# A gated-attention and two-MLP kernel: the second weight set's remainder moves from TensorE to VectorE, and two rules of its planner change

## The chip, the cores and the metric

One core of one Trainium2 chip. The metric is the device time of one execution in microseconds. Three engines matter: TensorE (PE; its weight loads are a row of their own, PEld), VectorE (DVE) and ScalarE (ACT). SyncE (SP) only issues the DMAs.

## The reference

The input is a batch of 4, with 8 heads, 768 steps and a head width of 48. A linear recurrence with a complex gate comes first, then two MLPs one after the other, all in float32.

```
a_re, a_im = a_re * scale, a_im * scale      # scale = min(|a|, 0.999) / (|a| + 1e-6)
for t in range(768):
    S_re, S_im = ar*S_re - ai*S_im + outer(k[t], v[t]), ar*S_im + ai*S_re
    y[t] = q[t] @ S_re
x = y as (3072, 384)
h = x @ w_in;   x   = (h * tanh(softplus(h))) @ w_out        # w_in 384 x 2048
h = x @ w2_in;  out = (h * clip(h + 3, 0, 6) / 6) @ w2_out
```

## The kernel before

**Numbers as pairs.** Every float32 factor of the MLPs is held as two float16 tiles, `hi` (the rounded value) and `lo` (the remainder), and each product is three float16 matmuls (hi·hi, hi·lo, lo·hi). This holds for the weights (`w1i`, `w1o`, `w2i`, `w2o`: first and second MLP, in and out) as for the activations (`x_hi`/`x_lo`, `gh`/`gl`).

**Weights (`weights`, L828 to L848).** The weights arrive as float64 bit patterns and are converted in pieces of 128x512, 24 pieces for the first set (`w1i`, `w1o`) and 24 for the second (`w2i`, `w2o`). One piece takes a DMA, ACT L840, DVE L841 and L842 (they make the float32 value `tf`), ACT L843 (`hi`), then PE L845 and L846 and ACT L847 for the remainder:

```
        act(out=hi, in_=tf, func=AF.Copy, scale=s * 2.0 ** -128)
        pw = ps_h.tile([128, 512], F32, name="pw", tag="ph")
        mm(pw, small, tf, start=True, stop=False)
        mm(pw, minus[:, idx % 2], hi, start=False, stop=True)
        act(out=lo, in_=pw, func=AF.Copy, scale=s / SWO)
```

`small` and `minus` are scaled identities, so that `pw` is the value minus `hi`. For the second set the value lies in a tile `wt` of one buffer.

**Blocks and stages.** The 3072 tokens are cut into 12 blocks of 256. For a block b there are: E`b` (`elementwise`, `spread`, `tail`: the gates' running products on DVE and ACT in the tiles `inp`, `tq` and `pp`, then 12 DMAs that lay the results out anew as `rq` and `rk`); C`b` (`chunks`: two chunks of 128 steps, each with the transposes `pk`, the scores `psc`, in `advance` the state update `pu`, in `second` the outputs `py` in two parts (scores by values at L785, queries by the old state `sd` at L791), and in `turn` the transposes `pst`; at last `x1conv` forms `x_hi` and `x_lo`); the first MLP's layer (0, b) and the second's (1, b). A layer is 8 pairs of column tiles; a pair is 18 matmuls into `ph` (L889), one ScalarE/VectorE treatment (`act1` with four ACT steps and DVE L912, or `act2` with one ACT step and DVE L919), the split into `gh` (ACT L925) and `gl` (DVE L926), and 18 matmuls out (L902).

**Order of the layers.** (0,0), (0,1), (1,0), (0,2), (1,1), (0,3), and so on. The second set of weights is converted during (0,0) and (0,1); it is needed from (1,0) on.

**What sets the order.** `survey` and `plan` arrange all instructions on each engine: `survey` gives each a cost and lists what it must wait for, `plan` sweeps over them forwards and backwards, and the resulting row of each engine is fixed. Two of its rules matter here. `runs` are groups of matmuls with 64 output partitions (`pu`, `py`) that are kept together as one piece; a group ends where the tile written or the kind of the first operand changes (the test at L332). And `lag` (L384) is the time that the plan leaves between an instruction and one that waits for it: 900 ns behind a DMA, 6000 ns more where the waiting one is part of the weights' range check (label "G").

Of the kernel before, what the change touches and what calls it, by code (L numbers as in the profile page):

```python
# [10 lines left out]
F32 = mybir.dt.float32  # L11
# [3 lines left out]
AF = mybir.ActivationFunctionType  # L15
ALU = mybir.AluOpType
# [23 lines left out]
SLACK = {}  # L40
AHEAD = 0.17
MARGIN = 6000.0
SIGN = -2147483648
BUT_SIGN = 0x7FFFFFFF
LOW3 = 2.0 ** -29 * (1.0 - 2.0 ** -20)
# [5 lines left out]
SWO = 2.0 ** 5  # L51
# [192 lines left out]
def survey(instructions, first, labels):  # L244
# [14 lines left out]
    ops, label, tags = [], [], [x[1] for x in labels]  # L259
# [8 lines left out]
            label.append(tags[j])  # L268
    n = len(ops)
    preds = [dict() for _ in range(n)]  # L270
    runs, where, stage = [], {}, {}
    seen, users, rows = {}, {}, {}
    cost, issue, dma, port = [0.0] * n, [0.0] * n, [False] * n, [False] * n
    for k, i in enumerate(ops):
        aps = [(x, False) for x in i.ins if hasattr(x, "bass_ap")] + [(x, True) for x in i.outs if hasattr(x, "bass_ap")]
        tiles = [(x.bass_ap, mybir.dt.size(x.dtype), wr) for x, wr in aps]
        out = tiles[-1][0]
        for ap, width, wr in tiles:
            name = ap.tensor.name
            tag = getattr(ap.tensor, "tag", None)  # L280
            if tag is None:
                continue
            key = tag.split("_")[0] if not tag.startswith("x2_") else tag[:5]
            wr = wr or key in ("oa", "oB")
            whole = key in ("ph", "oa", "oB", "pa", "td")
            box = (0, 128, 0, 1 << 30)
            if not whole:
                p0, lo = divmod(ap.offset, ap.ap[0][0])
                lo += sum(s * (c - 1) for s, c in ap.ap[1:] if s < 0)
                hi = lo + sum(abs(s) * (c - 1) for s, c in ap.ap[1:]) + 1  # L290
                box = (p0, p0 + ap.ap[0][1], lo * width, hi * width)
            if name not in seen:
                seen[name], users[name] = [], []
                row = rows.setdefault(tag, [])
                if row:
                    preds[k][users[row[-1]][0]] = ops[users[row[-1]][0]].engine != i.engine
                row.append(name)
                old = len(row) - 1 - bufs.get(key, 1)
                if old >= 0:
                    for p in users[row[old]]:  # L300
                        preds[k][p] = True
            if users[name]:
                first_use = users[name][0]
                if first_use != k:
                    preds[k].setdefault(first_use, ops[first_use].engine != i.engine)
            users[name].append(k)
            keep = []
            for b, p, pw in seen[name]:
                if (wr or pw) and b[0] < box[1] and box[0] < b[1] and b[2] < box[3] and box[2] < b[3] and p != k:
                    preds[k][p] = preds[k].get(p, False) or pw or ops[p].engine != i.engine  # L310
                if wr and p != k and box[0] <= b[0] and b[1] <= box[1] and box[2] <= b[2] and b[3] <= box[3]:
                    continue
                if not wr and not pw and b == box and tag.startswith("w"):
                    continue
                keep.append((b, p, pw))
            keep.append((box, k, wr))
            seen[name] = keep
        free = max(size(ap.ap) for ap, _, _ in tiles)
        if "DMA" in type(i).__name__:
            dma[k] = True  # L320
            count = math.prod(c for _, c in out.ap)
            issue[k] = 450.0 if out.ap[0][1] > 32 else 625.0
            cost[k] = count * tiles[-1][1] / (360.0 if min(adjacent(ap) * w for ap, w, _ in tiles) >= 2048 else 175.0)
        elif i.engine == tensor:
            passes = 1 if tiles[0][1] == 2 else 2 if i.is_transpose else 4
            cost[k] = passes * size(out.ap) / 2.4 + (2.0 if passes == 1 else 8.0)
            if out.ap[0][1] == 64:
                cost[k] = 115.0
                last = runs[-1][-1] if runs else -1
                if runs and label[last] == label[k] and out.tensor.name == where[last] and stage[last] == tiles[0][0].tensor.tag.split("_")[0]:  # L330
                    runs[-1].append(k)
                else:  # L332
                    runs.append([k])
                    cost[k] += 250.0
                where[k], stage[k] = out.tensor.name, tiles[0][0].tensor.tag.split("_")[0]
        elif i.engine == vector:
            fast = type(i).__name__ == "InstMemset" or (type(i).__name__ == "InstTensorScalarPtr" and len(tiles) == 2)
            steps = max(abs(ap.ap[-1][0]) * w for ap, w, _ in tiles)
            cost[k] = 66.0 + free / (1.92 if fast else 0.96) * (1.5 if steps >= 32 else 1.0)
            sb = [ap for ap, _, wr in tiles if not wr and getattr(ap.tensor, "tag", "").split("_")[0] not in ("ph", "oa", "oB", "pa")]  # L340
            port[k] = len(sb) >= 2 or fast
        elif i.engine == scalar:
            psum = tiles[0][0].tensor.tag.split("_")[0] in ("ph", "oa", "oB", "pa")
            cost[k] = (51.0 if psum else 94.0) + 93.0 * sum(size(ap.ap) == 1 for ap, _, _ in tiles) + free / 1.2
        else:
            cost[k] = 46.0 + free * 2.083
            port[k] = True
# [4 lines left out]
def plan(ops, label, preds, cost, issue, dma, port, runs):  # L352
# [5 lines left out]
    last = -1  # L358
    for k in range(n):
        if ops[k].engine == tensor and label[k][0] == "M":  # L360
            if last >= 0:
                chain[last] = k
            last = k
# [19 lines left out]

    def lag(p, k):  # L384
        if dma[p]:
            return 900.0 + (MARGIN if label[k] == "G" else 0.0)
        return after[ops[p].engine] if preds[k][p] and not (ops[p].engine == ops[k].engine == tensor) else 0.0

    rank = [0.0] * n
# [88 lines left out]
def fast_path(ctx, tc, a, out, flag):  # L478
    nc = tc.nc
    mm = nc.tensor.matmul  # L480
    act = nc.scalar.activation
    tt = nc.vector.tensor_tensor
    ts = nc.vector.tensor_scalar
    stt = nc.vector.scalar_tensor_tensor
# [12 lines left out]
    ps_h = ctx.enter_context(tc.tile_pool(name="ps_h", bufs=PHB, space=PSUM))  # L497
# [7 lines left out]
            name=nc.get_next_instruction_name(),  # L505
# [42 lines left out]
    minus = const.tile([128, 2, 128], F16, name="minus")  # L548
    small = const.tile([128, 128], F32, name="small")
# [278 lines left out]
    def weights(idx, nm, s, o):  # L828
# [9 lines left out]
        tf = t.bitcast(F32)  # L838
        hi, lo = W[nm][0][:, o:o + 512], W[nm][1][:, o:o + 512]
# [1 line left out]
        stt(t, hw, 3, lw, op0=ALU.logical_shift_left, op1=ALU.bitwise_or)  # L841
        stt(t, hw, BUT_SIGN, t, op0=ALU.bitwise_or, op1=ALU.bitwise_and)  # L842
        act(out=hi, in_=tf, func=AF.Copy, scale=s * 2.0 ** -128)  # L843
        pw = ps_h.tile([128, 512], F32, name="pw", tag="ph")
        mm(pw, small, tf, start=True, stop=False)  # L845
        mm(pw, minus[:, idx % 2], hi, start=False, stop=True)  # L846
        act(out=lo, in_=pw, func=AF.Copy, scale=s / SWO)  # L847
        yield  # L848

    def weight_guard():  # L850
# [11 lines left out]
    stage = iter(range(24))  # L862
# [116 lines left out]
    start = len(nc.cur_bb.bb.instructions)  # L979
# [133 lines left out]
```

## Time and profile before

| | us |
|---|---|
| median of 3 runs | 1038.88 |
| lowest and highest of them | 1034.57, 1039.21 |
| the profiled execution | 1037.71 |
| its span in the trace | 1035.8 |
| TensorE busy in it | 968.7 |
| VectorE busy | 800.5 |
| ScalarE busy | 675.2 |

The span is what the trace covers; 1.9 us lie around it. Busy times are unions over an engine's own instructions, and the three engines work side by side, so that they add up to more than the span. An engine's share of the whole span is a mean over stages that differ: the weights' conversion and the first blocks stand at the start, and from (1,0) on blocks and layers repeat.

### The profile page before, as it was taken

The numbers are of one execution on the slowest core, as the hardware profiler recorded it, in microseconds if no ns is written. First come the engines' busy times: TensorE is split into PE (matmuls) and PEld (weight loads), VectorE is DVE, ScalarE is ACT, GpSimd is POOL, SyncE is SP. The second block draws the span as 40 slices with busy tenths as digits, with TensorE's granted clock in tenths as the row PEclk, the third lists the DMA queues.
The fourth block names the chain that finished last, engine by engine and source line by source line (L and its number), as shares of the span: only waits on it lengthen the run. The fifth ranks groups of instructions, "written<-read, shape, count | busy, mean of one in ns | idle before, by whom it ended". The sixth has DMA issues, their size and how long they took to land.

```text
span 1035.8 us, 21145 instructions
## 1 busy us (share of the span) xinstructions
PE 968.7 (94%) x8719; PEld 817.9 (79%) x8719; DVE 800.5 (77%) x1455; ACT 675.2 (65%) x1181; POOL 0.9 (0%) x7
## 2 busy tenths in 40 slices
PE   3576889999999999999999999999999999999998
PEld 1144577788888888887888888888887988988887
DVE  7978779979699695895797996895994996654532
ACT  7865789955856846846747747747647747637532
POOL 0000000000000000000000000000000000000000
PEclk9888999999999999999999999999999999999999
DMA  9771854550615126029027146327237227222000
GB/s 357 287 137 45 157 169 143 135 106 24 119 37 100 43 68 112 1 68 166 3 91 158 53 114 151 98 89 156 84 108 131 83 85 155 85 69 77 22 16 19
DMA packets 58681, 106.64 MB, mean 103 GB/s; under 512 B 6482, under 2 KB 40018, under 8 KB 58578
## 3 DMA queue, kind: packets, MB, share of 16 engines
q1 hardware_dynamic: 53586, 100.50, 39.0%
q10 hardware_dynamic: 4992, 4.72, 1.4%
q8 instruction: 70, 1.15, 0.5%
q14 instruction: 33, 0.27, 0.1%
HBM read 80.35 MB, written 4.79 MB: 82 GB/s over the span
## 4 chain that ended last, share of the span: by engine, by line
PE 60%; DVE 16%; ACT 10%; DMA 9%; SPq 2%; issue 2%; ACTq 0%; DVEq 0%
PE ph L889 25%; PE oa L902 16%; PE oB L902 8%; DMA rk<-tq 5%; PE psc L739 3%; PE pw L845 2%; SPq L713 2%; PE py L785 1%; DMA rq<-inp 1%; DVE gl L926 1%; DMA yr<-yr 1%; PE py L791 1%; ACT s L909 1%; DVE s L919 1%; DVE tq L682 1%
## 5 line engine op out<-in xcount | busy, mean ns | idle before, releaser
L926 DVE TENSOR_TENSOR gl<-s,gh 128x512 f16<-128x512 f32 x192 | 131.9, 687 | 53.4 <-ACT gh L925 52.8
L925 ACT ACTIVATE gh<-s 128x512 f16<-128x512 f32 x192 | 120.1, 625 | 76.0 <-DVE s L919 64.2
L889 PE MATMUL ph<-x_hi,w1i_hi 128*128 128x256 f16 x576 | 158.4, 276 | 6.3 <-ACT x_hi L817 3.7
L889 PE MATMUL ph<-x_lo,w1i_hi 128*128 128x256 f16 x576 | 158.6, 276 | 0.2 <-DVE x_lo L818 0.2
L889 PE MATMUL ph<-x_hi,w1i_lo 128*128 128x256 f16 x576 | 158.3, 275 | 0.0
L889 PE MATMUL ph<-x_hi,w2i_hi 128*128 128x256 f16 x576 | 157.1, 273 | 0.0
L889 PE MATMUL ph<-x_hi,w2i_lo 128*128 128x256 f16 x576 | 157.1, 273 | 0.0
L889 PE MATMUL ph<-x_lo,w2i_hi 128*128 128x256 f16 x576 | 157.1, 273 | 0.0
L889 PEld LDWEIGHTS <-w1i_hi 128*128 128x128 f16 x1152 | 113.9, 99 | 23.8 <-issue 8.5
L902 PEld LDWEIGHTS <-w1o_hi 128*128 128x128 f16 x1152 | 113.2, 98 | 20.6 <-issue 6.2
L902 PEld LDWEIGHTS <-w2o_hi 128*128 128x128 f16 x1152 | 112.2, 98 | 16.2 <-issue 4.0
L889 PEld LDWEIGHTS <-w2i_hi 128*128 128x128 f16 x1152 | 111.9, 98 | 14.7 <-issue 2.7
L918 ACT ACTIVATE s<-ph,half 128x512 f32<-128x512 f32 x96 | 65.5, 682 | 80.7 <-PE ph L889 80.6
L902 PE MATMUL oa<-gl,w1o_hi 128*128 128x256 f16 x384 | 105.1, 274 | 4.2 <-DVE gl L926 4.0
L902 PE MATMUL oa<-gh,w1o_hi 128*128 128x256 f16 x384 | 105.2, 274 | 3.2 <-ACT gh L925 3.2
L902 PE MATMUL oa<-gl,w2o_hi 128*128 128x256 f16 x384 | 104.7, 273 | 0.7 <-DVE gl L926 0.7
L902 PE MATMUL oa<-gh,w1o_lo 128*128 128x256 f16 x384 | 105.0, 273 | 0.0
L902 PE MATMUL oa<-gh,w2o_hi 128*128 128x256 f16 x384 | 104.7, 273 | 0.0
L902 PE MATMUL oa<-gh,w2o_lo 128*128 128x256 f16 x384 | 104.7, 273 | 0.0
L919 DVE SCALAR_TENSOR_TENSOR s<-s,ph 128x512 f32<-128x512 f32 x96 | 65.5, 682 | 43.1 <-ACT s L918 42.8
L912 DVE SCALAR_TENSOR_TENSOR s<-s,ph 128x512 f32<-128x512 f32 x96 | 65.6, 684 | 42.6 <-ACT s L911 42.1
L908 ACT ACTIVATE s<-ph 128x512 f32<-128x512 f32 x96 | 56.4, 588 | 24.2 <-PE ph L889 20.8
(153 smaller groups left out, 2076.7 us busy)
## 6 DMA issues: line engine op xcount, KB each, us to landing
wst<-in_w2i_dram SPq DMA_DIRECT2D x24, 512.0 KB
wst<-in_w2o_dram SPq DMA_DIRECT2D x24, 512.0 KB
rq<-inp SPq DMA_DIRECT2D x72, 128.0 KB
rk<-tq SPq DMA_DIRECT2D x72, 128.0 KB
inp<-in_ga_dram SPq DMA_DIRECT2D x11, 768.0 KB
inp<-in_qk_dram SPq DMA_DIRECT2D x11, 768.0 KB
vt<-in_vt_dram SPq DMA_DIRECT2D x24, 256.0 KB
wst<-in_w1i_dram SPq DMA_DIRECT2D x12, 512.0 KB
```

Of the source, the lines that this page charges most:

```text
L682: tt(pl2(tq, 0, 2, 1, w), pl2(pp, 0, 2, 1, w), k_.unsqueeze(1).to_broadcast([128, 2, cols]), op=ALU.mult)
L713: nc.sync.dma_start(out=dst[pl * D + 16 * i:pl * D + 16 * (i + 1), :, :w], in_=vw(src, planes[pl], w)[:, i],)
L739: mm(p[:, hh], rk[:, 4 * g + hh, cs], rq[:, 4 * g + hh, cs], start=True, stop=True)
L845: mm(pw, small, tf, start=True, stop=False)
L889: mm(ph[:, j * w:(j + 1) * w], wt[:, sl], xx[:, k], start=(j == 0 and i == 0), stop=(i == 3 * KD - 1), skip_group_check=True)
L902: mm(po[m], wt[:, sl], gg[:, j * w:(j + 1) * w], start=(ft == 0 and i == 0 and m == 0), stop=(ft == KF - 1 and i == 2), skip_group_check=True)
L908: act(out=s, in_=ph, func=AF.Exp, scale=1.0 / H1)
L912: stt(s, s, 2.5, ph, op0=ALU.subtract, op1=ALU.mult)
L918: act(out=s, in_=ph, func=AF.Relu, scale=1.0 / (6.0 * H2), bias=half)
L919: stt(s, s, 1.0, ph, op0=ALU.min, op1=ALU.mult)
L925: act(out=gh[:, :w], in_=s, func=AF.Copy)
L926: tt(gl[:, :w], s, gh[:, :w], op=ALU.subtract)
```

## The change

It does three things. The second set's remainder (`idx >= 2`) is formed by one VectorE instruction from the value and `hi`, in place of two matmuls and a ScalarE copy; the first set is as before. A group of 64-partition matmuls now goes on as long as no other TensorE instruction stands between in the program, so that `pu` and both parts of `py` are one piece. And `lag` puts 2500 ns on top of the 900 where an instruction of E2 or a later block waits for a DMA of an E stage.

```
+NEXT = 2500.0
...
+            narrow = out.ap[0][1] == 64
             passes = 1 if tiles[0][1] == 2 else 2 if i.is_transpose else 4
             cost[k] = passes * size(out.ap) / 2.4 + (2.0 if passes == 1 else 8.0)
-            if out.ap[0][1] == 64:
+            if narrow:
                 cost[k] = 115.0
                 last = runs[-1][-1] if runs else -1
-                if runs and label[last] == label[k] and out.tensor.name == where[last] and stage[last] == tiles[0][0].tensor.tag.split("_")[0]:
+                if runs and tensor_ops[-1] == last:
                     runs[-1].append(k)
                 else:
                     runs.append([k])
                     cost[k] += 250.0
-                where[k], stage[k] = out.tensor.name, tiles[0][0].tensor.tag.split("_")[0]
+            tensor_ops.append(k)
...
-            return 900.0 + (MARGIN if label[k] == "G" else 0.0)
+            return 900.0 + (MARGIN if label[k] == "G" else NEXT if label[k][0] == label[p][0] == "E" and label[k] not in ("E0", "E1") else 0.0)
...
-        pw = ps_h.tile([128, 512], F32, name="pw", tag="ph")
-        mm(pw, small, tf, start=True, stop=False)
-        mm(pw, minus[:, idx % 2], hi, start=False, stop=True)
-        act(out=lo, in_=pw, func=AF.Copy, scale=s / SWO)
+        if idx < 2:
+            pw = ps_h.tile([128, 512], F32, name="pw", tag="ph")
+            mm(pw, small, tf, start=True, stop=False)
+            mm(pw, minus[:, idx % 2], hi, start=False, stop=True)
+            act(out=lo, in_=pw, func=AF.Copy, scale=s / SWO)
+        else:
+            stt(lo, tf, s * 2.0 ** -128, hi, op0=ALU.mult, op1=ALU.subtract)
```

What this makes of the order is shown at three places. The changed kernel's line numbers are 2 to 5 higher: its L843, L844 are the old L841, L842; L917, L924, L931 the old L912, L919, L926; L907 the old L902; L591 the old L589; the new instruction is L852.

VectorE, where E2 ends; before (L682 is its last instruction there):

```order
L668 TENSOR_TENSOR inp<-pp,inp 128x2x768
L912 SCALAR_TENSOR_TENSOR s_1808<-s_1808,ph 128x512
L841 SCALAR_TENSOR_TENSOR wt<-wst 128x512
L842 SCALAR_TENSOR_TENSOR wt<-wst,wt 128x512
L926 TENSOR_TENSOR gl<-s_1808,gh 128x512
L912 SCALAR_TENSOR_TENSOR s_1866<-s_1866,ph 128x512
L676 TENSOR_TENSOR tq<-tq 128x768
L673 TENSOR_REDUCE gm<-tq 128x1
L678 SCALAR_TENSOR_TENSOR tq<-tq 128x768
L926 TENSOR_TENSOR gl<-s_1866,gh 128x512
L680 TENSOR_TENSOR inp<-inp,tq 128x768
L919 SCALAR_TENSOR_TENSOR s_1935<-s_1935,ph 128x512
```

The same place with the change:

```order
L917 SCALAR_TENSOR_TENSOR s_1800<-s_1800,ph 128x512
L852 SCALAR_TENSOR_TENSOR w2i_lo<-wt,w2i_hi 128x512
L931 TENSOR_TENSOR gl<-s_1745,gh 128x512
L843 SCALAR_TENSOR_TENSOR wt<-wst 128x512
L678 TENSOR_TENSOR tq<-tq 128x768
L844 SCALAR_TENSOR_TENSOR wt<-wst,wt 128x512
L675 TENSOR_REDUCE gm<-tq 128x1
L680 SCALAR_TENSOR_TENSOR tq<-tq 128x768
L670 TENSOR_TENSOR inp<-pp,inp 128x2x768
L682 TENSOR_TENSOR inp<-inp,tq 128x768
L931 TENSOR_TENSOR gl<-s_1800,gh 128x512
L684 TENSOR_TENSOR tq<-pp,inp 128x1536
```

Ahead of E2's last instruction stand, before, all 48 pieces' L841 and L842 and 17 pairs' L912/L919; with the change 40 pieces' L843 and L844, 15 of the 24 new L852, 16 pairs' L917, and 2 reductions fewer. So 9 pieces of the second set are finished after E2 instead of ahead of it.

TensorE in the first chunk of C2, around the state update; before:

```order
L902 MATMUL oa<-gl,w2o_hi 128x256
L756 MATMUL pu<-kt,vt 64x96 x8
L739 MATMUL psc<-rq,rk 128x128
L902 LDWEIGHTS w2o_lo
L902 MATMUL oa<-gh,w2o_lo 128x256
```

With the change:

```order
L907 MATMUL oa<-gh,w2o_hi 128x256
L758 MATMUL pu<-kt,vt 64x96 x8
L787 MATMUL py<-am,vt 64x128 x8
L793 MATMUL py<-rq,sd 64x128 x8
L907 LDWEIGHTS w2o_hi
```

The outputs' matmuls have moved up to the state update. Before, `py` stood directly behind `pu` in 4 of 20 chunks, and the second part of `py` behind the first in 3 of 20; with the change in all 20 each.

ScalarE at the start of E6 (L589 and L590, the gates' squares, which write `tq` once the DMAs of `spread` have read it); before, behind the last use of `tq` by E5 (L671):

```order
L671 ACTIVATE tq<-tq 128x768
L792 ACTIVATE yr<-py 128x4x128
L918 ACTIVATE s_4131<-ph,half 128x512
L925 ACTIVATE gh<-s_4131 128x512
L817 ACTIVATE x_hi<-yr 128x768
L918 ACTIVATE s_4175<-ph,half 128x512
L925 ACTIVATE gh<-s_4175 128x512
L908 ACTIVATE s_4456<-ph 128x512
L589 ACTIVATE tq<-inp 128x768
```

With the change, the last rows ahead of it:

```order
L930 ACTIVATE gh<-s_4627 128x512
L915 ACTIVATE s_4674<-s_4674,fifth 128x512
L916 ACTIVATE s_4674<-s_4674 128x512
L930 ACTIVATE gh<-s_4674 128x512
L913 ACTIVATE s_4721<-ph 128x512
L591 ACTIVATE tq<-inp 128x768
```

Between E5's L671 and E6's L589 there were 7 ScalarE instructions, now there are 20; from E6 on there are 20 to 27 where there were 7 to 11.

## Rows read from the trace of the kernel before

**Rows 1.** The page, part 1: busy us (share of the span) xinstructions.

```profile
PE 968.7 (94%) x8719; PEld 817.9 (79%) x8719; DVE 800.5 (77%) x1455; ACT 675.2 (65%) x1181; POOL 0.9 (0%) x7
```

**Rows 2.** Stages: from:to, length; PE, PEld, DVE, ACT, POOL busy; clock; DMA; GB/s.

```profile
64.00:209.00 145.00, 125.13 (x963) 92.14 (x962) 122.30 (x224) 115.89 (x213) 0.00 (x0) 0.95 0.51 131
...
131.00:204.00 73.00, 71.37 (x565) 54.25 (x566) 66.36 (x122) 69.20 (x129) 0.00 (x0) 0.98 0.50 143
204.00:278.00 74.00, 72.48 (x693) 63.97 (x692) 59.16 (x105) 47.38 (x83) 0.00 (x0) 1.00 0.41 84
204.00:1036.00 832.00, 814.08 (x7737) 718.55 (x7735) 627.46 (x1130) 512.63 (x884) 0.00 (x0) 0.99 0.36 85
```

**Rows 3.** The tile pw alone, on PE: from:to, length, busy, clock, DMA, GB/s.

```profile
85.00:212.00 127.00, 35.53 (x72) 0.95 0.53 136
```

**Rows 4.** Groups by line and shape: busy us, mean ns, idle before and its ends.

```profile
L926 DVE TENSOR_TENSOR gl<-s,gh 128x512 f16<-128x512 f32 x192 | 131.9, 687 | 53.4 <-ACT gh L925 52.8
...
L841 DVE SCALAR_TENSOR_TENSOR wt<-wst 128x512 int32<-128x512 int32 x24 | 16.5, 688 | 5.2 <-ACT wst L840 3.1 <-PE pw L845 1.9 <-ACT w2o_hi L843 0.2
...
L843 ACT ACTIVATE w2i_hi<-wt 128x512 f16<-128x512 f32 x12 | 7.5, 623 | 5.0 <-DVE wt L842 5.0
```

**Rows 5.** Waits of DVE from 64 to 209: us in total, times, longest.

```profile
DVE tq L591 <- ACT tq L590: 9.1, 2, 6.3
DVE wt L841 <- ACT wst L840: 3.1, 2, 2.7
...
DVE wt L841 <- PE pw L845: 1.9, 4, 1.3
...
DVE gl L926 <- ACT gh L925: 0.7, 1, 0.7
```

**Rows 6.** Timeline, PE: state update and outputs joined, then apart (start us, us).

```profile
136.74 0.88 PE L756 MATMUL pu<-kt,vt 128*64 128x96 f32 x16
137.45 1.04 PE L785 MATMUL py<-am,vt 128*64 128x128 f32 x16
138.32 1.04 PE L791 MATMUL py<-rq,sd 96*64 96x128 f32 x16
...
225.19 0.88 PE L756 MATMUL pu<-kt,vt 128*64 128x96 f32 x16
226.00 0.49 PE L739 MATMUL psc<-rq,rk 96*128 96x128 f32 x2
...
227.42 0.27 PE L902 MATMUL oa<-gh,w2o_hi 128*128 128x256 f16 x1
227.53 0.27 PE L902 MATMUL oa<-gl,w2o_hi 128*128 128x256 f16 x1
227.73 1.09 PE L785 MATMUL py<-am,vt 128*64 128x128 f32 x16
228.76 0.28 PE L902 MATMUL oa<-gh,w2o_lo 128*128 128x256 f16 x1
```

**Rows 7.** Timeline: last DVE instruction of E2 and E3, first PE matmuls behind.

```profile
207.29 1.75 DVE L682 TENSOR_TENSOR tq<-pp,inp 128x1536 f32<-128x1536 f32 x1
...
246.62 0.27 PE L889 MATMUL ph<-x_hi,w1i_hi 128*128 128x256 f16 x1
...
270.92 1.75 DVE L682 TENSOR_TENSOR tq<-pp,inp 128x1536 f32<-128x1536 f32 x1
...
321.91 0.27 PE L889 MATMUL ph<-x_hi,w1i_hi 128*128 128x256 f16 x1
```

**Rows 8.** Waits from 204 to the end, PE, then ACT behind the spread DMAs.

```profile
PE oa L902 <- ACT gh L925: 2.1, 2, 1.5
...
PE pu L756 <- DVE am L741: 0.7, 1, 0.7
...
ACT tq L589 <- DMA rk<-tq: 9.2, 8, 2.4
...
ACT tq L590 <- DMA rk<-tq: 8.1, 8, 1.9
```

More of the change, by code (lines that the diff above doesn't have):

```diff
@@ L270, in survey @@
     preds = [dict() for _ in range(n)]
-    runs, where, stage = [], {}, {}
+    runs, tensor_ops = [], [-2]
     seen, users, rows = {}, {}, {}
```

## The prediction

> **What bounds the kernel now.** I read the page first, then the busy times by stage, then the waits and the timeline inside the stages where an engine has room. The page gives TensorE 968.7 of a span of 1035.8 us, VectorE 800.5, ScalarE 675.2 [rows 1]. The stages show that this mean hides two regimes [rows 2]. From 204 us on TensorE works 814.08 of 832 us; VectorE (627.46) and ScalarE (512.63) have room, and whatever TensorE is spared there comes off the end. From 64 us (first matmuls of C0) to 209 us (E2's last VectorE instruction, at 207.29 for 1.75 [rows 7]) all three are loaded: TensorE 125.13 of 145, VectorE 122.30, ScalarE 115.89; and in its second half, 131 to 204, they are busy 71.37, 66.36 and 69.20 of 73. TensorE comes first there, but the others stand 4 to 7 us behind it. This is where the second set is converted.
>
> The sum is made against the profiled execution, 1037.7 us (the span and 1.9 around it), 1.2 below the median of the three runs.
>
> **The second set's remainder.** Removed are TensorE's matmuls on the tile `pw`: 35.53 us between 85 and 212 [rows 3], with 24 ScalarE copies. Added are 24 VectorE instructions 128x512 that read a float32 and a float16 tile and write float16. Their nearest row is L926, with the same shapes and types, at 687 ns [rows 4]: 16.5 us. If TensorE alone set this stage, 35.5 us would come off. It doesn't: without them it has some 90 of 145 us of work, and VectorE's 122.3 become the bound. So the stage is worked out from VectorE.
>
> Ahead of E2's last instruction the new order has 15 of the new instructions (+10.3 us at 0.687), 8 pieces' L841 and L842 fewer (16 x 0.688 = -11.0 [rows 4]) and one L919 fewer (-0.7, taken at L926's price, same shape). Two reductions fewer I leave out. VectorE's work there is then 122.3 - 1.4 = 120.9 us: nearly unchanged, because the planner puts 9 pieces behind E2. What can shrink are VectorE's waits, 145 - 122.3 = 22.7 us. The largest are 9.1 us for the first gate squares of E1 and E2, 6.3 of them one wait, 3.1 for ScalarE's L840 and 1.9 for TensorE to release `wt` [rows 5]. The last goes with the matmuls. Ahead of E2's L591 stand 7 VectorE instructions more than before, of about 0.6 us each as they follow one another, which covers 4.2 of the 6.3; ahead of E1's there are 3 more, 1.9 us. Of the 3.1 I take half, since ScalarE loses the copies. Together 9.5 us.
>
> A new wait comes in: each L852 needs ScalarE's `hi` (L843) of the same piece. What stands behind it on VectorE are the pairs' L912 and L926, for which TensorE waits. The trace has no such wait; the nearest from below is `gl` waiting for `gh`, 0.7 us over the 15 that this stage has, 0.05 each [rows 5]; from above the whole copy, 0.623 us [rows 4]. In the new order one to four VectorE instructions stand between a piece's L844 and its L852 in 11 of the 15 cases, more in the rest, so I take 0.17, nearer the lower row: 15 x 0.17 = 2.5 us (bounds 0.7 and 9.3).
>
> The stage becomes shorter by 1.4 + 9.5 - 2.5 = **8.4 us**. Bounds: 18 us if all of the named waits go but the lower price of the new one; -7 (longer) if none goes and each new one costs a whole copy.
>
> **What the 9 late pieces do.** They give VectorE 9 x 0.687 + 16 x 0.688 = 17.2 us between E2 and E3, and E3's end now stands behind 33 pairs instead of 29 (4 x 1.37 = 5.5 us more). E2's end to E3's end took 63.6 us before [rows 7], of which VectorE was idle about 13: it had 59.16 of 74 in that stretch [rows 2]. If 10 are used up, E3 ends 22.7 - 10 - 8.4 = 4.3 us later than before. From E3's end (272.7) to the first matmul of (0,3) at 321.91 there are 49.2 us; from E2's end to (0,2) at 246.62 the same way took 37.6 [rows 7]. So 11.6 us are spare, and (0,3) can start 7.3 us earlier instead of 8.4: **+1 us** (bounds 0 and 11, where nothing is used up).
>
> **State update and outputs as one piece.** Apart, `pu` begins 0.20 us behind the float16 matmul before it and is followed after 0.81; `py` begins after 0.20 and is followed after 1.03. Float16 matmuls follow each other every 0.11. Joined, the steps are 0.71 and 0.87 [rows 6]. A joint saves 0.09 at the entry and 0.10 behind `pu`, or 0.16 behind `py`: 0.19 and 0.25 us. Before, 4 and 3 of 20 were joined; now all. 16 x 0.19 + 17 x 0.25 = 7.3 us, all but 0.2 of it behind 204 us, where TensorE sets the end: **-7.1 us**. What may cost it: the piece starts when its last input is there, `sd` and both `am` now for the state update too. One such wait stands in the trace, 0.7 us for `am` [rows 8]. The planner puts layer matmuls ahead of the piece, and I cost it at nothing; without that cover it is the third rival.
>
> **The margin.** It moves the next block's L589 and L590 back by about 13 ScalarE instructions from E6 on. They wait 9.2 and 8.1 us for the spread DMAs [rows 8], but ScalarE has room; only what TensorE waits for `gh` behind them can come back, 2.1 us in all [rows 8]. I take **-1 us** (bounds -2 and +3, where a later start lets an E end late).
>
> **The sum.** -8.4 + 1 - 7.1 - 1 = -15.5: 1037.7 - 15.5 = **1022 us**. This case holds while the stage gains 3 to 15 us, the latter being all waits of the four rows; with the margin's bounds that is 1013 to 1031.
>
> **Rivals.** (1) *TensorE's matmuls count nearly in full.* For it: TensorE idles 1.6 us in 131 to 204 [rows 2]. Against it: VectorE's 120.9 us of work in what would have to be a stage of 110. In full it gives 1037.7 - 35.5 - 7.1 - 1 = 994; half-way from my forecast, 1008.
>
> (2) *They were hidden.* If VectorE and ScalarE set the stage already, only the joints count: 1037.7 - 7.1 = 1030.6. For it: their 66.36 and 69.20 of 73. Against it: VectorE's waits, which are for the others. The Trainium skill (Perfetto Trace Analysis, section Identifying the Most-Contended Engine) says that the busy share of matmuls is a bad measure of TensorE and its weight loads a better one, and that the engine of the highest occupancy binds. By it 131 to 204 belongs to ScalarE, weight loads being busy 54.25 of 73, and the sum is this rival's; against it the trace shows matmuls starting every 0.11 us without a gap.
>
> (3) *The joined pieces stand waiting.* At 0.7 us for each of 20 chunks [rows 8] TensorE gives back 14 us: 1022 + 14 = 1036, no change.
>
> (4) *VectorE becomes the bound: slower.* In order, it stands at each L852 until ScalarE has made `hi`, and keeps its old waits. At 0.623 us each [rows 4], E2 ends -1.4 + 9.3 = 7.9 us later, E3 a further 22.7 + 5.6 - 10 = 18.3, less 11.6 spare: (0,3) starts 14.6 later, and with the joints behind it (about 5.4) the end is 1037.7 + 9.2 = 1047. With the old waits it ends above 1044 from about 0.5 us per L852 on. Against it: ScalarE loses 24 copies and the order leaves work between.
>
> **How the numbers follow.** A measurement of this kernel can tell about 0.5% from no change, 5.2 us: faster is below 1033.7, slower above 1044.1, counted from the median. My case has 0.55, rival 1 (994 to 1013) 0.13, rival 2 0.16, rival 3 0.10, rival 4 0.06. The first three cases named are faster: 0.84; same 0.10, slower 0.06. From 1007 to 1035 leaves out the farther half of rival 1, rival 4 and part of rival 3, somewhat under 0.2. My own case is 1013 to 1031.
>
> **What would show it.** Right: E2's last VectorE instruction at about 200; VectorE's waits from 64 to there near 15 us, with L852 behind L843 at 2 to 4 of them; TensorE under 75% busy in the second half of the stage; (0,3) starting near 314; `pu`, `py` and `py` at steps of 0.71 and 0.87; L589's wait for the DMAs under 2 us from E6 on. Wrong: TensorE's waits behind 204 growing beyond 17 us (rival 3), L852 waiting over 0.4 us each or (0,3) starting after 322 (rival 4), E2 ending at 209 (rival 2) or before 190 (rival 1).

## The result and the profile after

The changed kernel takes 998.8 us (median of 4 runs, 996.9 to 999.51) beside 1037.16 for the kernel before on the same chip (4 runs, 1034.57 to 1039.21): a ratio of 0.960, 95% interval 0.9566 to 0.9633. It is faster by 38.4 us by the medians, and by 39.1 between the two profiled executions, where 15.5 were forecast, and lies below the range.

Page of the kernel after, part 1, busy us (share of the span) xinstructions:

```profile
PE 935.5 (94%) x8647; PEld 810.6 (81%) x8647; DVE 809.3 (81%) x1479; ACT 664.4 (67%) x1157; POOL 0.9 (0%) x7
```

TensorE has 33.2 us less than in [rows 1], close to the matmuls taken away, and VectorE only 8.8 more. The span fell from 1035.8 to 996.5.

Two points of the trace divide this: the first matmul of layer (1,1) and TensorE's last matmul. The way to the first one (the **head**, conversion and first blocks) went from 278.1 to 258.2 us, 19.9 shorter. The stretch **behind** it went from 752.7 to 732.6 us, 20.1 shorter. What follows the last matmul grew by 0.7.

Stages of the kernel after (columns as in [rows 2]):

```profile
64.00:189.20 125.20, 103.98 (x921) 86.17 (x920) 116.60 (x219) 97.94 (x177) 0.00 (x0) 0.92 0.46 120
131.00:204.00 73.00, 64.26 (x573) 55.16 (x572) 68.29 (x129) 55.30 (x101) 0.00 (x0) 0.96 0.48 109
189.20:268.60 79.40, 76.65 (x715) 67.83 (x714) 73.28 (x132) 57.27 (x101) 0.00 (x0) 0.97 0.50 109
258.00:991.00 733.00, 729.94 (x7049) 654.56 (x7046) 573.88 (x1034) 466.82 (x807) 0.00 (x0) 1.00 0.37 90
```

Its timeline: the last VectorE instruction of E2 and E3, the first matmuls of (0,2), (1,1) and (0,3), and the joined pieces in a chunk:

```profile
187.47 1.75 DVE L684 TENSOR_TENSOR tq<-pp,inp 128x1536 f32<-128x1536 f32 x1
...
226.07 0.27 PE L894 MATMUL ph<-x_hi,w1i_hi 128*128 128x256 f16 x1
...
258.21 0.27 PE L894 MATMUL ph<-x_hi,w2i_hi 128*128 128x256 f16 x1
...
266.82 1.76 DVE L684 TENSOR_TENSOR tq<-pp,inp 128x1536 f32<-128x1536 f32 x1
...
299.80 0.27 PE L894 MATMUL ph<-x_hi,w1i_hi 128*128 128x256 f16 x1
...
350.03 0.27 PE L907 MATMUL oa<-gh,w2o_lo 128*128 128x256 f16 x1
350.23 0.88 PE L758 MATMUL pu<-kt,vt 128*64 128x96 f32 x16
350.94 1.04 PE L787 MATMUL py<-am,vt 128*64 128x128 f32 x16
351.81 1.05 PE L793 MATMUL py<-rq,sd 96*64 96x128 f32 x16
352.79 0.28 PE L907 MATMUL oB<-gh,w2o_hi 128*128 128x256 f16 x1
```

E2 ends at 189.2 (209.0 before, [rows 7]), (0,2) starts 20.5 us earlier, E3 ends only 4.1 earlier and (0,3) starts 22.1 earlier. So E3 was not what (0,3) stood behind: from E3's end it took 49.2 us before and takes 31.2 now.

VectorE's waits from 64 to 189.2, which answer to [rows 5], then TensorE's from 258 to the end, to [rows 8] (us in total, times, longest):

```profile
DVE am L743 <- PE psc L741: 2.4, 1, 2.4
DVE s L917 <- ACT s L916: 1.2, 1, 1.2
DVE tq L668 <- ACT tq L667: 1.0, 1, 1.0
DVE tq L593 <- ACT tq L592: 1.0, 1, 1.0
DVE w2i_lo L852 <- ACT w2i_hi L845: 0.8, 1, 0.8
DVE w2o_lo L852 <- ACT w2o_hi L845: 0.4, 1, 0.4
DVE gl L931 <- ACT gh L930: 0.4, 1, 0.4
```

```profile
PE ph L894 <- DVE x_lo L820: 1.2, 3, 0.7
PE oa L907 <- DVE gl L931: 0.9, 3, 0.5
PE oa L907 <- ACT gh L930: 0.7, 1, 0.7
```

VectorE's 9.1 us for the gates' squares are 1.0, and the waits for `wst` and for TensorE to release `wt` are gone; one for TensorE's `psc` stays. The new instruction waits 1.2 us in all. Behind (1,1) TensorE's idle time in the timeline is 2.7 us instead of 11.0. That is 8.3 of the 20.1 us there. A further 3.3 are float16 matmuls that ran at the lower of TensorE's two clock levels before and do not now; some 7 are the joints; 1.6 lie at the transposes `pst` and the scores `psc`, which I did not follow further.

### The profile page after: what moved, and what is told of

The parts are those of the page before. It is cut to its first block, busy times and chain, and to the rows that moved or that the text cites. A ratio compares the mean times of both kernels' runs of the same rounds, so it can differ in the third digit from the quotient of the medians.

```text
span 996.5 us, 20985 instructions
## 1 busy us (share of the span) xinstructions
PE 935.5 (94%) x8647; PEld 810.6 (81%) x8647; DVE 809.3 (81%) x1479; ACT 664.4 (67%) x1157; POOL 0.9 (0%) x7
## 4 chain that ended last, share of the span: by engine, by line
PE 59%; DVE 13%; ACT 3%; DMA 1%; issue 1%; SPq 0%; ACTq 0%; DVEq 0%
PE ph L894 27%; PE oa L907 18%; PE oB L907 9%; PE psc L741 2%; DVE gl L931 1%; DVE s L924 1%; DVE am L743 1%; PE py L787 1%; DVE mm L617 1%; DMA out_dram<-s 1%; PE py L793 1%; DVE tq L653 1%; DVE inp L653 1%; PE pk L734 1%; DVE gm L862 1%
## 5 line engine op out<-in xcount | busy, mean ns | idle before, releaser
L931 DVE TENSOR_TENSOR gl<-s,gh 128x512 f16<-128x512 f32 x192 | 131.3, 687 | 52.6 <-ACT gh L930 52.0
L907 PEld LDWEIGHTS <-w1o_hi 128*128 128x128 f16 x1152 | 113.3, 98 | 17.4 <-issue 3.6
L907 PEld LDWEIGHTS <-w2o_hi 128*128 128x128 f16 x1152 | 112.5, 98 | 13.0 <-issue 0.9
L907 PE MATMUL oa<-gl,w1o_hi 128*128 128x256 f16 x384 | 105.5, 275 | 4.2 <-DVE gl L931 4.2
L907 PE MATMUL oa<-gh,w1o_hi 128*128 128x256 f16 x384 | 105.4, 274 | 2.7 <-ACT gh L930 2.7
L907 PE MATMUL oa<-gh,w1o_lo 128*128 128x256 f16 x384 | 105.5, 275 | 0.0
L907 PE MATMUL oa<-gh,w2o_hi 128*128 128x256 f16 x384 | 105.0, 273 | 0.0
L907 PE MATMUL oa<-gh,w2o_lo 128*128 128x256 f16 x384 | 104.8, 273 | 0.0
L907 PE MATMUL oa<-gl,w2o_hi 128*128 128x256 f16 x384 | 104.8, 273 | 0.0
L917 DVE SCALAR_TENSOR_TENSOR s<-s,ph 128x512 f32<-128x512 f32 x96 | 65.5, 683 | 42.1 <-ACT s L916 41.7
L924 DVE SCALAR_TENSOR_TENSOR s<-s,ph 128x512 f32<-128x512 f32 x96 | 65.4, 682 | 36.2 <-ACT s L923 35.9
```

The lines of the kernel that those rows point to most:

```text
L907: mm(po[m], wt[:, sl], gg[:, j * w:(j + 1) * w], start=(ft == 0 and i == 0 and m == 0), stop=(ft == KF - 1 and i == 2), skip_group_check=True)
L917: stt(s, s, 2.5, ph, op0=ALU.subtract, op1=ALU.mult)
L924: stt(s, s, 1.0, ph, op0=ALU.min, op1=ALU.mult)
L931: tt(gl[:, :w], s, gh[:, :w], op=ALU.subtract)
```

## The experiments

Where a table gives them, *head* is the time to the first matmul of (1,1), *behind* the stretch from it to TensorE's last matmul, *idle* TensorE's idle time in that stretch, and *ACT waits* the sum of ScalarE's waits there for a DMA that are over 0.5 us each; all four are read from the timeline of one profiled execution, the time is the median. The profiled execution lies within 2.5 us of the median, but for next4000 (3.6 us above it) and act_copies_value (4.5 above it).

### Each part alone, and two together

From the kernel before: the new branch `if idx < 2 ... else: stt(lo, ...)` alone; the new test for `runs` alone; `NEXT` in `lag` alone; the first two.

> Only the second set's remainder goes to VectorE; pieces and margin are as before. Theory A (each part works by a mechanism of its own): 18 to 22 us faster, all of it ahead of the first matmul of (1,1), at 278 us before and near 258 here; behind it idle time (11 us before) and half-clock matmuls (3.3 us before) of TensorE stay. Rival B (any change of costs makes the planner lay out another order, and what the changed kernel gained behind 258 is that order's luck): the gain behind the first matmul of (1,1) is as likely 0 as 10 us, so that the whole comes anywhere from 12 to 32 us.

> Only the state update and both parts of the outputs become one piece. Theory A: 33 joints of 0.19 to 0.25 us, 7 us faster, spread evenly behind 204 us, and TensorE's idle time behind 278 us stays near 11 us. Rival B: idle time behind 278 us changes by 4 us or more in either direction, and the whole lies anywhere from 12 us faster to 3 us slower.

> Only the 2500 ns behind the E stages' DMAs are added to the plan. Theory A: ScalarE's waits for the spread DMAs (15 us behind 278 us before) fall under 3 us, and with them TensorE's idle time behind 278 us falls from 11 to about 4 us and its half-clock stretches (3.3 us) go: 8 to 11 us faster. Theory as forecast: 1 us faster, the idle time having other causes. Rival B: ScalarE's waits fall, but TensorE's idle time does not follow them.

> The remainder on VectorE and the joined pieces, without the margin. Theory A: 20 + 7 = 27 us faster, with 10 us or more of TensorE idle behind the first matmul of (1,1). Rival B: as fast as the change as a whole (38 us faster), the idle time being gone without the margin.

| kernel | us | ratio, 95% | head | behind | idle | ACT waits |
|---|---|---|---|---|---|---|
| before | 1038.7 | | 278.1 | 752.7 | 11.0 | 25.4 |
| remainder_alone | 1024.2 | 0.985 (0.9812 to 0.9886) | 259.0 | 756.7 | 14.5 | 24.3 |
| joints_alone | 1035.1 | 0.995 (0.993 to 0.9974) | 280.3 | 744.5 | 12.6 | 23.3 |
| margin_alone | 1040.6 | 1.001 (0.9987 to 1.0041) | 282.5 | 749.9 | 8.6 | 17.4 |
| remainder_joints | 1012.9 | 0.972 (0.9687 to 0.9759) | 260.8 | 744.6 | 8.9 | 15.2 |
| changed | 998.8 | 0.960 (0.9566 to 0.9633) | 258.2 | 732.6 | 2.7 | 10.9 |

The remainder shortens the head by 19 us whether the joints are there or not, more than double the 7.4 forecast (8.4 less 1). Alone it takes 14.5 us off the time, less than the 18 to 22 expected, for the stretch behind grows by 4.0. The joints shorten the stretch behind by 8 and 12 us, the time by 3.6 and 11.3. The margin alone does nothing to the time; but on top of the other two the step from 1012.9 to 998.8 is its own, 14 us in this order of the planner's, where 1 was forecast.

### How much is luck of the order

The planner's order changes with any of its numbers. Two of them were moved a little, in remainder_joints, in the changed kernel and in the kernel before; no operation changes.

```
-AHEAD = 0.17
+AHEAD = 0.16
```

```
-    after = {tensor: 183.0, vector: 145.0, scalar: 160.0, pool: 117.0}
+    after = {tensor: 183.0, vector: 150.0, scalar: 160.0, pool: 117.0}
```

> Remainder and joined pieces without the margin, and a number of the planner without a meaning of its own here (how far it waits for a better instruction, 0.17) set to 0.16. Theory M (the margin works by sparing ScalarE's waits for the spread DMAs): within 4 us of remainder and joints at 0.17, about 1011, since those waits stay. Theory L (which order comes out is luck, worth several us): anywhere from 996 to 1022.

> Remainder and joined pieces without the margin; the planner's time from a VectorE instruction to one on another engine is 150 ns in place of 145, another change without a meaning. Theory M: about 1011, within 4 us. Theory L: anywhere from 996 to 1022.

> The whole change with 0.16 in place of 0.17. Theory M: within 4 us of the changed kernel, about 998, TensorE's idle time behind the first matmul of (1,1) at most 5 us. Theory L: anywhere from 994 to 1015, with idle time from 3 to 15 us.

> The whole change with 150 ns in place of 145. Theory M: about 998, within 4 us. Theory L: anywhere from 994 to 1015. Beyond the single values: if both kernels with the margin lie below both without it, the margin works whatever the order; if they mix, it doesn't by itself.

> The kernel before with one of the planner's search weights at 0.16 instead of 0.17, which changes no operation, only the order that the planner finds. If the time depends on the order by several us, as it did with the remainder and joined pieces, 1030 to 1046 us; if the order before was a lucky one, above 1040 us; if an unlucky one, below 1035 us.

> The kernel before with the planner's figure for a wait on VectorE at 150 instead of 145, which changes no operation, only the order. As for the other: 1030 to 1046 us by the spread seen so far; both runs above 1040 us would say that part of the change's gain is the kernel before's good order, both below 1035 us the reverse.

| kernel | us | ratio, 95% | head | behind | idle | ACT waits |
|---|---|---|---|---|---|---|
| rj_ahead16 | 1007.2 | 0.969 (0.9663 to 0.9724) | 262.1 | 738.5 | 5.8 | 13.0 |
| rj_dve150 | 1009.7 | 0.972 (0.9691 to 0.9758) | 261.6 | 741.0 | 8.1 | 14.9 |
| all_ahead16 | 1005.4 | 0.967 (0.9643 to 0.9704) | 265.9 | 732.4 | 3.2 | 5.9 |
| all_dve150 | 1007.8 | 0.970 (0.9665 to 0.9728) | 266.7 | 734.5 | 3.5 | 9.2 |
| before_ahead16 | 1041.0 | 1.001 (0.9978 to 1.0041) | 284.9 | 750.6 | 9.5 | 20.4 |
| before_dve150 | 1041.0 | 1.001 (0.9984 to 1.0045) | 279.4 | 753.9 | 11.2 | 26.3 |

The kernel before is an ordinary draw: three orders lie within 2.4 us. The changed kernel is a good one, the best of three (998.8, 1005.4, 1007.8). The stretch behind hardly differs among the three (732.4 to 734.5); its luck lies in the head (258.2 against 265.9 and 266.7). By the means of three orders each (1040.2 and 1004.0) the change is worth 36 us. With the margin the stretch behind is shorter by 12.0, 6.1 and 6.5 in the three pairs, so its part there is no luck. The head takes most of it back in two of them: the time falls by 14.1, 1.8 and 1.9 us. By the test set for all_dve150 the times mix (1005.4 and 1007.8 with the margin, 1007.2 and 1009.7 without), so that on the whole time the margin does not work whatever the order; the mean of the three pairs is 5.9 us.

### The margin with either part

The margin added to joints_alone and to remainder_alone, in the kernel before:

```
-        return 900.0 + (MARGIN if label[k] == "G" else 0.0)
+        return 900.0 + (MARGIN if label[k] == "G" else NEXT if label[k][0] == label[p][0] == "E" and label[k] not in ("E0", "E1") else 0.0)
```

> Joined pieces and the margin, with the second set's remainder by TensorE as before. If the margin adds to the joints here too, the stretch from block 1 of set 2 to the end goes from 744.5 (joints alone) to 730 to 738 us, and the time from 1035 to 1021 to 1031 us, by where the head comes out (278 to 286 us). If not, 742 us or more and 1033 us or more.

> The remainder by VectorE and the margin behind the gates' loads, without the joined pieces. If the margin takes out waits behind block 1 of set 2 whatever the pieces are, the stretch from there to the end goes from 756.7 (remainder alone) to 746 to 752 us with under 8 us of idle TensorE, and the time from 1024 to 1012 to 1020 us. If it needs the joined pieces, the stretch stays above 753 us and the time above 1020 us.

| kernel | us | ratio, 95% | head | behind | idle | ACT waits |
|---|---|---|---|---|---|---|
| joints_margin | 1019.9 | 0.982 (0.9786 to 0.9844) | 280.3 | 730.3 | 1.4 | 4.9 |
| remainder_margin | 1012.0 | 0.975 (0.9707 to 0.9796) | 259.8 | 743.3 | 5.7 | 8.6 |

The time of joints_margin came out 1 us below the first forecast, the stretch of remainder_margin 2.7. With joints the margin takes 14.2 us off the stretch behind and 15.2 off the time, with the remainder 13.4 and 12.2. It needs neither of them in particular. One way in which it can work shows in joints_alone between 404 and 415 us: ScalarE, VectorE, then TensorE in its timeline (start us, us, then [idle before <- what ended it]).

```profile
407.01 0.72 ACT L910 ACTIVATE s<-s,one 128x512 f32<-128x512 f32 x1
410.50 0.84 ACT L590 ACTIVATE tq<-inp 128x768 f32<-128x768 f32 x1 [2.76 <-DMA rk<-tq]
411.25 0.58 ACT L948 ACTIVATE s<-oa 128x512 f32<-128x512 f32 x1
411.72 0.38 ACT L948 ACTIVATE s<-oB 128x256 f32<-128x256 f32 x1
...
412.22 0.27 DVE L973 MEMSET oB<- 128x256 f32 x1 [5.00 <-ACT s L948]
...
412.55 0.27 PE L903 MATMUL oB<-gh,w1o_hi 128*128 128x256 f16 x1 [1.72 <-DVE oB L973]
```

ScalarE stands 2.76 us at the next block's square, until the DMAs have read `tq`. Behind it, in order, are the copies of a finished layer's `oa` and `oB`; VectorE waits for them to clear `oB`, and TensorE waits 1.72 us for that. The wait is listed under VectorE's `oB`, though neither VectorE nor ScalarE's work is its cause. TensorE's waits in joints_alone and in joints_margin, from (1,1) to the end (the four largest of each):

```profile
PE oa L903 <- ACT gh L926: 5.3, 4, 2.4
PE oB L903 <- DVE oB L973: 3.7, 4, 1.7
PE oa L903 <- DVE gl L927: 1.5, 5, 0.5
PE ph L890 <- ACT x_hi L818: 0.9, 1, 0.9
```

```profile
PE oa L904 <- ACT gh L927: 0.8, 1, 0.8
PE pst L800 <- DVE am L743: 0.2, 1, 0.2
PE oa L904 <- DVE gl L928: 0.2, 1, 0.2
PE ph L891 <- DVE x_lo L820: 0.2, 1, 0.2
```

The waits for `gh`, `oB` and `gl` go together once ScalarE's waits for DMAs fall from 23.3 to 4.9 us. Only the wait at 412.55 was followed back; that the others had the same cause is not shown. In the kernel before the margin alone only brought these from 25.4 to 17.4 and the stretch down by 2.8; why less there was not settled.

### A larger and a smaller margin

```
-NEXT = 2500.0
+NEXT = 4000.0
```

The second with 1500.0.

> The changed kernel with 4000 ns of margin instead of 2500. If the margin works by taking away ScalarE's waits for the E blocks' DMAs (10.9 us behind block 1 of set 2 with 2500, 15.2 without), these fall below 8 us, TensorE's idle time behind there stays under 4 us and the stretch is 729 to 734 us; the time is 996 to 1008 us by where the order puts the head (258 to 267 us). If a larger margin makes the E blocks late, waits for rk and x_hi grow and the stretch is above 738 us.

> The changed kernel with 1500 ns of margin instead of 2500. If the margin's worth comes by degrees, ScalarE's waits for DMAs behind block 1 of set 2 are 9 to 15 us, TensorE's idle time there 3 to 8 us and the stretch 733 to 742 us; the time 998 to 1014 us with the head at 258 to 267 us. If 1500 ns cover the transfers as well as 2500, the stretch is 729 to 734 us.

| kernel | us | ratio, 95% | head | behind | idle | ACT waits |
|---|---|---|---|---|---|---|
| next1500 | 1010.0 | 0.970 (0.964 to 0.9768) | 262.8 | 739.1 | 6.9 | 7.6 |
| next4000 | 1013.7 | 0.975 (0.9688 to 0.9803) | 266.4 | 743.6 | 7.8 | 1.9 |

With 4000 ScalarE's waits are nearly gone, as expected, and yet TensorE is idle for longer; half of it stands in one row of its timeline:

```profile
290.91 0.87 PE L734 MATMUL pk<-cst,rk 96*128 96x96 f32 x4 [4.03 <-DMA rk<-tq]
```

Here TensorE itself waits for the `rk` of E3, which is late. That would be the other side of a margin: too small, ScalarE stands at a transfer and holds up what is queued behind it; too large, the block ends late. But the runs do not show it, for such a row stands in kernels without any margin too, as in the timeline of remainder_joints:

```profile
282.07 0.85 PE L733 MATMUL pk<-cst,rk 96*128 96x96 f32 x8 [3.08 <-DMA rk<-tq]
```

The same wait is 1.85 us in remainder_alone, 1.57 in rj_ahead16 and 1.46 in rj_dve150, all without the margin, 2.95 in next1500 and 3.63 in remainder_margin; the changed kernel has none over 0.15 for E3's `rk`. With one order each the two runs do not say which value is best. Nor does the sum of ScalarE's waits give TensorE's idle time: 10.9 goes with 2.7 in the changed kernel, 7.6 with 6.9 in next1500 and 1.9 with 7.8 in next4000.

### What in the remainder was worth 19 to 23 us

From joints_margin to the changed kernel only the remainder differs: the head goes from 280.3 to 258.2 and the time from 1019.9 to 998.8. The next two kernels give back one engine's relief each. In the changed kernel, TensorE forms the remainder and VectorE copies it:

```
-            stt(lo, tf, s * 2.0 ** -128, hi, op0=ALU.mult, op1=ALU.subtract)
+            pw = ps_h.tile([128, 512], F32, name="pw", tag="ph")
+            mm(pw, small, tf, start=True, stop=False)
+            mm(pw, minus[:, idx % 2], hi, start=False, stop=True)
+            ts(lo, pw, s / SWO, None, op0=ALU.mult)
```

> The changed kernel, but the second weight set's remainder is again formed by TensorE's two matmuls and copied out of PSUM by VectorE; ScalarE stays relieved, VectorE still has one instruction for it. Theory (in the way to block 1 of the second set TensorE's 35.5 us of matmuls were paid almost in full): the gain there goes, the first H of block 1 of set 2 stands at 276 to 285 us instead of 258, and the time is 1015 to 1028 us. Rival (the gain came from taking the copy off ScalarE): the first H stays at 256 to 266 us and the time at 997 to 1008 us.

In the other ScalarE has its copy back and VectorE nothing:

```
-            stt(lo, tf, s * 2.0 ** -128, hi, op0=ALU.mult, op1=ALU.subtract)
+            act(out=lo, in_=tf, func=AF.Copy, scale=s * 2.0 ** -139)
```

> The changed kernel, but the second set's low half is a ScalarE copy of the scaled value, with no subtraction: the remainder itself is left out. TensorE stays relieved of the matmuls, VectorE of the new instruction, and ScalarE has its copy back. Theory (with the matmuls gone VectorE, busy 116.6 of 125.2 us from 64 us on, sets the pace of the head): taking some 16 us off it brings the first H of block 1 of set 2 from 258 to 245 to 255 us and the time to 985 to 997 us. Rival (ScalarE's copy was what bounded the head): the first H goes back to 272 to 282 us and the time to 1012 us or more. Third (neither; the loads or the chain bound it now): no change within 4 us.

In the next two TensorE has its matmuls back beside VectorE's instruction, and nobody reads what they form. The first pair of matmuls is that of pe_unread; in pe_unread_wt the second pair stands in its place.

```
             stt(lo, tf, s * 2.0 ** -128, hi, op0=ALU.mult, op1=ALU.subtract)
+            pw = ps_h.tile([128, 512], F32, name="pw", tag="ph")
+            mm(pw, small, W["w1i"][0][:, 0:1024].bitcast(F32), start=True, stop=False)
+            mm(pw, minus[:, idx % 2], W["w1i"][0][:, 0:512], start=False, stop=True)
...
+            mm(pw, small, tf, start=True, stop=False)
+            mm(pw, minus[:, idx % 2], hi, start=False, stop=True)
```

> The changed kernel, and besides, for each piece of the second set, the two TensorE matmuls of the kernel before, on operands that have long been ready (weights of the first set) into a PSUM tile that nobody reads. TensorE has its 35.5 us of work back, but nobody waits for it. Theory A (it is TensorE's time that was paid): the first H of block 1 of set 2 goes from 258 to 276 to 286 us and the time to 1012 to 1022 us. Theory B (what was paid is the loop around the single buffer wt, which TensorE held until it had read it, and a copy behind TensorE): the first H stays at 256 to 267 us and the time at 997 to 1008 us.

> As the run before, but the two unread matmuls read the piece's own value in wt and its hi, so that TensorE also holds the single buffer wt, as in the kernel before; no copy waits behind it. Theory A: the same as the run before, within 4 us (276 to 286 us for the first H, 1012 to 1022 us). Theory B: 8 us or more longer than the run before.

| kernel | us | ratio, 95% | head | behind | E2 ends |
|---|---|---|---|---|---|
| changed | 998.8 | 0.960 (0.9566 to 0.9633) | 258.2 | 732.6 | 189.2 |
| act_copies_value | 999.9 | 0.961 (0.9544 to 0.9679) | 263.6 | 733.0 | 194.0 |
| pe_unread | 1015.4 | 0.976 (0.9735 to 0.9793) | 274.4 | 733.5 | 196.7 |
| pe_remainder_dve_copy | 1022.6 | 0.984 (0.9767 to 0.9905) | 285.9 | 729.9 | 218.0 |
| pe_unread_wt | 1025.7 | 0.987 (0.9836 to 0.9908) | 285.3 | 731.4 | 222.5 |

Stages: act_copies_value's way to E2's end, then pe_unread's second half, then the way to E2's end in pe_unread and in pe_unread_wt (columns as in [rows 2]):

```profile
64.00:194.00 130.00, 111.66 (x954) 93.01 (x953) 113.20 (x211) 106.92 (x199) 0.00 (x0) 0.88 0.47 116
```

```profile
131.00:204.00 73.00, 72.70 (x559) 54.10 (x556) 70.39 (x131) 58.59 (x104) 0.00 (x0) 1.00 0.48 121
```

```profile
64.00:196.70 132.70, 117.36 (x892) 86.53 (x892) 118.92 (x222) 98.75 (x174) 0.00 (x0) 0.92 0.49 125
```

```profile
64.00:222.50 158.50, 134.73 (x1025) 100.25 (x1023) 134.93 (x246) 108.53 (x194) 0.00 (x0) 0.91 0.45 116
```

Three readings follow.

- *VectorE's work alone does not set the head.* Without the 24 new instructions (16.5 us) the time is the same and the head no shorter, but 5.4 longer, within the spread of orders seen above and in an execution 4.5 us above its median. The Trainium skill (Perfetto Trace Analysis, section Identifying the Most-Contended Engine) says that the engine with the highest occupancy is the one to relieve first. In the changed kernel that is VectorE, 116.60 of 125.2 us; the measurement does not agree. ScalarE has 24 copies more in this run, so that a gain on VectorE and an equal loss on ScalarE are not ruled out.
- *TensorE's time alone is worth about 16 us.* Matmuls that nobody waits for bring the head from 258.2 to 274.4 and TensorE back to 72.70 of 73 us. That is a little under the 276 forecast, and some 45% of the 35.5 us added: without them TensorE stands for other things in the head, 6.8 us for `sT`, 4.0 for `x_lo` and 3.3 for `gl` from 64 to 189.2. The granted clock differs as well, 0.96 in the changed kernel from 131 to 204 and 1.00 in pe_unread; what that gave back was not separated.
- *Reading the piece's own value is worth about 11 us more,* by one pair of orders. When TensorE also reads `wt`, the head is 285.3, the same as when VectorE's copy waits behind it (285.9). I had set the two theories against each other; the runs show the first, and a cost beyond it. That the second cost is the single buffer `wt`, held by TensorE, is not shown. These are waits of pe_unread_wt from 64 to 222.5:

```profile
PE pw L854 <- DVE wt L844: 6.3, 4, 3.6
...
DVE w2i_lo L852 <- ACT w2i_hi L845: 6.8, 3, 3.6
...
DVE wt L843 <- PE pw L854: 0.5, 1, 0.5
```

TensorE stands 6.3 us until the value is in `wt`, with all that is queued behind that matmul, and VectorE 0.5 until TensorE has read it. The planner also lays out another order around both; a kernel with two buffers for `wt` would tell them apart and was not run. ScalarE's relief is not what counts: pe_remainder_dve_copy has it and gains nothing in the head, act_copies_value gives it back and keeps the time.

The two add to 27, while the remainder's part measured 19 to 23 in four pairs; orders differ by several us, and finer than this the split is open. What sets the head of the changed kernel, where no engine is full, is open too; the granted clock from 64 us to E2's end is 0.92 there and 0.95 before [rows 2], and what that costs was not worked out. No run beat the changed kernel.

## Why the prediction was wrong

**The direction was right, the size was not.** 39 us came for 15.5; 8.4 less 1 was forecast for the head, which gave 19.9, and 8.1 behind it, which gave 20.1.

**The step that failed first** is "without them it has some 90 of 145 us of work, and VectorE's 122.3 become the bound. So the stage is worked out from VectorE." The work was foreseen well enough: VectorE's work ahead of E2's end fell by 5.4 us (178.03 to 172.65 from the start on) where 1.4 was counted, and 1.9 of the rest are the two reductions I left out. But its waits were not its own. I took 9.5 of 22.7 us off them and added 2.5; they fell to 8.6. With TensorE's matmuls back but unread they are 13.8 us, and 23.6 when TensorE also reads `wt` (pe_unread and pe_unread_wt, one order each). So the larger part hung on the piece's way through TensorE, a smaller one on TensorE's time. The 9.1 us for the gates' squares fell to 1.0, of which I had covered 6.1 by counting instructions; in pe_unread they are 1.6, so TensorE's time alone does not explain them. An engine that is busy 122 of 145 us was read as one that needs most of the 145. The kernel without VectorE's instruction, as fast as the changed one, speaks against VectorE as the bound even afterwards. The stage's 19.8 us lie past the bound of 18 that I gave as the best case, and that bound does not follow from its terms: 1.4 and the named waits of 14.1, less 0.7, are 14.8 (the other bound is -7.9, not -7).

**The new wait** was sized at 2.5 us and measured 1.2, at 2 of the pieces, as the place in the order said.

**The nine late pieces** did what was worked out for E3: from E2's end to E3's it took 79.4 us, 76.3 by my sum. The price I put on it, +1, fell with the 37.6 us that I took (0,3) to need behind E3; it needed at most 31.2, so nothing was lost in this order. In seven other kernels with the remainder on VectorE TensorE stands 1.5 to 4.0 us for E3's `rk` between 278 and 291 us.

**The joints** were right in mechanism and nearly in size: steps of 0.71 and 0.87 in the timeline, all chunks joined, 8.2 us of the stretch behind when done alone, 7.1 forecast. In the other three pairs the stretch fell by 12.0, 10.7 and 19.6 us, TensorE's idle time and clock among it; with the idle time taken out the four pairs give 9.8, 6.5, 7.7 and 12.4. The rival that the pieces stand waiting fell: TensorE's matmuls wait nowhere for `am` or `sd` behind 258. The Trainium skill (TensorEngine Tiling (Array Packing), section Key Properties) says that a change of tiling mode drains TensorE; [rows 6] give 0.19 and 0.25 us for a joint here, and the runs bear that sum out. It is the 64 output partitions and not float32 that cost it: float32 matmuls with 128 output partitions (`psc`) begin 0.11 us behind a float16 matmul and are followed after 0.11, the median of some 100 such places each behind (1,1) in the kernel before.

**The margin** was mis-sized: 1 us forecast (-2 to +3), 6 to 14 measured behind (1,1) in five of six pairs, 2.8 in the sixth. On the whole time the pairs give 15.2, 14.1, 12.2, 1.9, 1.8 and -1.9, for in four of them the head grew by 0.8 to 5.1 us. I looked for TensorE's waits that name `gh` (2.1 us) where `oB`, `x_hi`, `s` and `gl` can stand behind ScalarE's waits for the transfers too: of 11.0 us of idle time in all 8.3 are gone in the changed kernel, with 3.3 of lower clock behind two of the gaps. That every gap had this cause is not shown. Ahead of the longest one before, 2.06 us at 487.39, VectorE works at a gate operation (L606, 1.76 us from 484.98), and ScalarE's last wait for a transfer ended at 476.43.

**Rivals.** The result lies in the range of the first, 994 to 1013, and its sign came (E2 ends at 189.2, before 190), but only half for its reason: of 35.5 us of matmuls 19 to 23 came back in the head, not all, and the margin and a good draw of the order made up the rest. TensorE was busy 64.26 of 73 us in the second half of the stage, 88%, where my case had under 75%. The second, that the matmuls are hidden by the others, is ruled out by pe_unread. The fourth, a bound by VectorE that makes the kernel slower, is ruled out by the result itself, with waits of 1.2 us for the new instruction.

## What to carry to other kernels

Before working a stage out from the next fullest engine, ask which of its waits hang on the engine that is being relieved; busy time and waits together are no lower bound of the stage. To price a wait on an in-order queue, follow everything queued behind it to the bounding engine, whatever name that engine's wait bears. Where a planner sets the order, draw a few orders before putting a few us down to an edit: here they differed by 2 to 9 us. And look at the whole time beside the stretch: what one stretch gains, another can give back.

## What was not expected of the hardware

A short gap on TensorE can cost more than itself. In the kernel before, TensorE's timeline behind an idle time of 2.06 us:

```profile
487.39 0.27 PE L889 MATMUL ph<-x_hi,w1i_hi 128*128 128x256 f16 x1 [2.06 <-DVE s L912]
487.50 0.37 PE L889 MATMUL ph<-x_lo,w1i_hi 128*128 128x256 f16 x1
487.67 0.42 PE L889 MATMUL ph<-x_hi,w1i_lo 128*128 128x256 f16 x1
487.88 0.42 PE L889 MATMUL ph<-x_hi,w1i_hi 128*128 128x256 f16 x1
488.09 0.42 PE L889 MATMUL ph<-x_lo,w1i_hi 128*128 128x256 f16 x1
```

From 487.67 to 490.87 the matmuls start every 0.21 us instead of 0.11, the lower level of the clock (1.2 instead of 2.4 GHz); the granted clock of 480 to 505 us is 0.93. The same happens behind a gap of 1.48 us at 790, and together it cost 3.3 us. Behind (1,1) the changed kernel has no gap over 0.7 us and a granted clock of 1.00. But the length of a gap does not decide it: joints_alone has gaps of 2.40 us at 572.18 and 1.72 at 412.55, with a granted clock of 1.00 from 560 to 600 and from 404 to 420. The Trainium skill (TensorE: Matmul & The Clock Gate, section What's actually happening) says that a gate sets the array's clock to one of these two levels by how busy TensorE has been of late; the trace agrees as to the two levels, with steps of 0.11 and 0.21 us, and has gaps ahead of both falls.
